# Attention into feed-forward on one core: the second batch's attention queued from a third of the first feed-forward on, ACT tables loaded ahead of use, three squares moved to Pool

## The chip, the cores and the metric

The kernel runs on 1 core of one Trainium2 chip. The metric is the device time of one execution in microseconds (us), as the median of several runs; lower is better. The profile is taken of one execution. Its span, from the first to the last instruction, is about 1.8 us shorter than the time of the same run. All runs quoted were classed as fast runs. With one core a single run says little about its state, so the granted TensorE clock is given where it matters.

Engines are named as in the profile: PE is TensorE (matmul), PEld its weight loads, ACT is ScalarE, DVE is VectorE, POOL is GpSimd, SP only issues DMAs here. "Batch 0" is the first of eight batches.

## The reference

Squared-relu attention on 8 batches of 12 heads, then RMS norm and a SwiGLU feed-forward on all tokens:

```python
# q, k, v: (8, 12, 448, 64)   w_gate, w_val: (768, 1536)   w_out: (1536, 768)
scores = matmul(q, k.T) / sqrt(64)
attn   = maximum(scores, 0) ** 2 / 448
x      = matmul(attn, v)                     # -> (3584, 768)
rms    = sqrt(mean(x * x, axis=-1) + 1e-6)
xn     = x / rms * rms_g
g      = xn @ w_gate
out    = (g * sigmoid(g) * (xn @ w_val)) @ w_out      # float32
```

## The kernel before

The kernel works batch by batch. It emits the attention and the norm of batch 0 alone; then, for each batch b, the feed-forward of b is the main list of units and the attention and norm of b+1 is the side list. `merge` writes both into one order. The schedule is manual: each engine executes its instructions in the order in which they were emitted, and waits (by semaphores) at the first one whose inputs are missing.

```python
def merge(main, side, head=0.0, tail=0.0):
    # side unit k is emitted once the main list has reached the share
    #   head + (1 - head - tail) * k / n   of its total cost
    ...

# emission of the loads, all from POOL's DMA queue, before any attention:
load("q", 0, ...); load("k", 0, ...); load("v", 0, ...)      # batch 0, in parts
for s in range(4):                       # gate and value weights, 4 slices each
    load_w("g", s)
    load_w("v", s)
for nm in ("q", "k", "v"):               # batch 1
    load(nm, 1)
load_wo(0, 2)
load_wo(1, 2)
# ... (cut)

def scores(b, j, cs):                    # head pair j, two of four chunks c
    # per chunk: two matmuls into psS (2 buffers), then
    #   r = relu(psS)  on ACT (on DVE for some c == 3);  later r = r * r
    eng = nc.gpsimd if square_on(b, j, c) == "pool" else nc.vector
    # the squares are kept in `pending` and emitted by flush() at the next scores()
    # ... (cut)

def attention(b):                        # the side units, in order (b = 0, 1)
    add(0.4, lambda: transposes(b, 0))   # PE transposes q, k of the pair (psT), DVE copies
    for j in range(6):
        add(0.5, scores(b, j, (0, 1)))
        add(0.4, transposes(b, j + 1))   # if j + 1 < 6
        add(1.2, scores(b, j, (2, 3)) and attend(b, j - 1))
    add(0.1, flush)
    add(0.8, attend(b, 5))
    # batch 0 has two keep_busy(2) per pair besides: matmuls on zeros

def norm(b):
    # six matmuls of ones with x*x -> psSS
    nc.scalar.activation(out=rstd[:], in_=psSS[:], func=ACT.Sqrt, ...)
    nc.vector.reciprocal(out=rstd[:], in_=rstd[:])
    for kt in range(6):
        nc.vector.scalar_tensor_tensor(out=xn[:, kt, :], ...)   # x * g * rstd

def ffn(b):      # 12 x (gate psG, value psV: six matmuls each), then the output
    # units psO: 3 pairs of (512, 256 columns) for even b, 4 for odd b
    # ... (cut)

keep_busy(16)
for fn in merge([], attention(0) + [(1.1, lambda: norm(0))]):
    fn()
for b in range(8):
    side = attention(b + 1) + [norm(b + 1)]
    main = ffn(b)
    # loads of batch b + 2 from POOL, DMA transposes of it from SP (cut)
    for fn in merge(main, side, 0.0, 0.15):
        fn()
```

The pieces above are abridged from the kernel; the exact text follows.

Of the kernel before, what the change touches and what calls it, by code (L numbers as in the profile page):

```python
# [8 lines left out]
FP32 = mybir.dt.float32  # L9
# [3 lines left out]
ACT = mybir.ActivationFunctionType  # L13
# [4 lines left out]
def merge(main, side, head=0.0, tail=0.0):  # L18


    total = sum(c for c, _ in main)
    if not main:
        return [f for _, f in side]
    out, done, k = [], 0.0, 0
    n = len(side)
    for c, f in main:
        while k < n and done >= total * (head + (1.0 - head - tail) * k / n):
            out.append(side[k][1])
            k += 1
        out.append(f)  # L30
        done += c
    out.extend(f for _, f in side[k:])
    return out
# [3 lines left out]
def kernel(  # L37
# [11 lines left out]
    nc = tc.nc  # L49
    P = nc.NUM_PARTITIONS  # L50
# [13 lines left out]
    const = ctx.enter_context(tc.tile_pool(name="consts", bufs=1))  # L64
# [20 lines left out]
    def load(nm, b, h0=0, h1=H):  # L85
        runs = nm == "v" or b < PE_T
        if (nm, b) not in ld:
            shape = [PC, H, NCH * D] if runs else [PC, NCH, H * D]
            ld[nm, b] = ldpool.tile(shape, BF16, name=nm + "b", tag=nm + "b")
        t = ld[nm, b]  # L90
        src = src_of[nm][b, h0:h1]
        if runs:
            nc.gpsimd.dma_start(out=t[:, h0:h1, :], in_=src.rearrange("h (p c) d -> p h (c d)", c=NCH))  # L93
        else:
            nc.gpsimd.dma_start(  # L95
                out=t[:].rearrange("p c (h d) -> p c h d", d=D)[:, :, h0:h1, :],
                in_=src.rearrange("h (p c) d -> p c h d", c=NCH),
            )
# [4 lines left out]
    def transpose_dma(b):  # L103
        new_qkT(b)
        for ti, nm in enumerate(("q", "k")):
            for c in range(NCH):
                nc.sync.dma_start_transpose(
                    out=qkT[b][:, :, ti, c * PC : (c + 1) * PC], in_=ld[nm, b][:, c, :]
                )
# [7 lines left out]
    def load_w(which, s):  # L117
        dst, src = {"g": (wg_sb, moe_w_gate), "v": (wv_sb, moe_w_val)}[which]
        nc.gpsimd.dma_start(
            out=dst[:, :, s * FS : (s + 1) * FS],  # L120
            in_=src.rearrange("(kt p) f -> p kt f", p=P)[:, :, s * FS : (s + 1) * FS],
        )

    def load_wo(s, n):
        w = FT // n
        nc.gpsimd.dma_start(
            out=wo_sb[:, s * w : (s + 1) * w, :],
            in_=moe_w_out.rearrange("(fk p) m -> p fk m", p=P)[:, s * w : (s + 1) * w, :],
        )
# [14 lines left out]
    masks.make_identity(nc, ident[:])  # L144
    eps_col = const.tile([P, 1], FP32, name="eps_col", tag="eps_col")
    nc.vector.memset(eps_col[:], eps)
    g_sb = wpool.tile([P, KT], FP32, name="g_sb", tag="rmsg")
    nc.sync.dma_start(out=g_sb[:], in_=moe_rms_g.rearrange("(kt p) -> p kt", p=P))
    load("q", 0, 2, 6)
# [5 lines left out]
    for s in range(NSL):  # L155
        load_w("g", s)
        load_w("v", s)
    for nm in ("q", "k", "v"):
        load(nm, 1)
    load_wo(0, 2)  # L160
    load_wo(1, 2)


    xTs = {}

# [18 lines left out]
        return "dve" if c == 3 and (b or j % 2) else "act"  # L184

    def square_on(b, j, c):
        return "dve"

    def flush():
        while pending:  # L190
# [2 lines left out]
    def scores(b, j, cs):  # L193
        pss = []
        for c in cs:
            psS = ps_s.tile([PC, 2, 512], FP32, name="psS", tag="psS")
            for hh in range(2):
                prt = slice(hh * D, (hh + 1) * D)
                nc.tensor.matmul(  # L199
                    out=psS[:, hh, :S],  # L200
                    lhsT=qkT[b][prt, j, 1, c * PC : (c + 1) * PC],
                    rhs=qkT[b][prt, j, 0, :],
                    start=True,
                    stop=True,
                )
            pss.append(psS)
        squares = []
        for c, psS in zip(cs, pss):
            r = apool.tile([PC, 2, S], BF16, name="r", tag="r")
            if relu_on(b, j, c) == "dve":  # L210
                nc.vector.tensor_relu(out=r[:], in_=psS[:, :, :S])  # L211
            else:
                nc.scalar.activation(out=r[:], in_=psS[:, :, :S], func=ACT.Relu)  # L213
            eng = nc.gpsimd if square_on(b, j, c) == "pool" else nc.vector
            squares.append(
                lambda r=r, eng=eng: eng.tensor_tensor(out=r[:], in0=r[:], in1=r[:], op=ALU.mult)  # L216
            )
            rsq[b, j, c] = r
        flush()
        pending.extend(squares)  # L220
# [25 lines left out]
    def attention(b):  # L246
        units = []

        def add(cost, *fns):
            units.append((cost, lambda: [f() for f in fns]))  # L250

        if b < PE_T:
            add(0.4, lambda: transposes(b, 0))
        for j in range(HP):
            add(0.5, lambda j=j: scores(b, j, (0, 1)))
            if b < PE_T and j + 1 < HP:
                add(0.4, lambda j=j: transposes(b, j + 1))
            if b == 0:
                add(0.3, lambda: keep_busy(2))
            add(1.2, lambda j=j: scores(b, j, (2, 3)), lambda j=j: j and attend(b, j - 1))  # L260
            if b == 0:
                add(0.3, lambda: keep_busy(2))
        add(0.1, flush)
        add(0.8, lambda: attend(b, HP - 1), flush)
        return units
# [4 lines left out]
    def norm(b):  # L270
        psSS = ps_m.tile([P, S], FP32, name="psSS", tag="mm")
        for kt in range(KT):
            nc.tensor.matmul(  # L273
                out=psSS[:], lhsT=ones_bf[:], rhs=x2s[b][:, kt, :],
                start=(kt == 0), stop=(kt == KT - 1),
            )
        rstd = npool.tile([P, S], FP32, name="rstd", tag="rstd", bufs=1)
        nc.scalar.activation(  # L278
            out=rstd[:], in_=psSS[:], func=ACT.Sqrt, scale=1.0 / float(DM), bias=eps_col[:]
        )  # L280
        nc.vector.reciprocal(out=rstd[:], in_=rstd[:])  # L281
        xn = npool.tile([P, KT, S], BF16, name="xn", tag="xn")
        for kt in range(KT):
            nc.vector.scalar_tensor_tensor(  # L284
                out=xn[:, kt, :], in0=xTs[b][:, kt, :], scalar=g_sb[:, kt : kt + 1], in1=rstd[:],
                op0=ALU.mult, op1=ALU.mult,
            )
        xns[b] = xn
        if b % 2 == 0:
            hTs[b // 2] = hpool.tile([P, FT, 2 * S], BF16, name="hT", tag="hT")  # L290
# [49 lines left out]
    def ffn(b):  # L340
        units = []
        for fb in range(FT):
            units.append((1.13, lambda fb=fb: gate(b, fb)))
            units.append((1.13, lambda fb=fb: value(b, fb)))
        full = S // P
        for t in range(full) if b % 2 == 0 else range(full, NT):
            units.append((2.56, lambda t=t: outproj(b // 2, t, 0, 512)))
            units.append((1.28, lambda t=t: outproj(b // 2, t, 512, DM - 512)))
        return units

    keep_busy(16)
    for fn in merge([], attention(0) + [(1.1, lambda: norm(0))]):
        fn()
    for b in range(B):
        side = []
        if b + 1 < B:
            side = attention(b + 1) + [(1.1, lambda b=b: norm(b + 1))]
        main = ffn(b)
        if b + 2 < B:
            for nm in ("q", "k", "v"):  # L360
                load(nm, b + 2)
            at = len(main) * 2 // 3
            main[at:at] = [(0, lambda b=b: transpose_dma(b + 2))]
        for fn in merge(main, side, 0.0, 0.15):
            fn()


# [28 lines left out]
```

## Time and profile before

| | before |
|---|---|
| time, median of 3 runs | 487.74 us (487.48 to 487.85) |
| span of the profiled run (its time 487.05) | 485.3 us |
| PE busy | 459.0 us |
| psSS of norm 0 starts | 32.91 us |
| first gate matmul (psG) starts | 48.62 us |
| granted PE clock 0.5 or falling to it | 38.0 to about 51.8 us |

The page's first part gives busy time by engine, with the share of the span and the number of instructions:

```profile
PE 459.0 (95%) x2856; PEld 220.2 (45%) x2872; DVE 284.2 (59%) x452; ACT 253.8 (52%) x372; POOL 50.8 (10%) x45
```

PE is the engine that bounds the kernel. The table of windows of the kernel before shows where it is not yet full. Its columns are the window, its length, then for each engine the busy us and the number of instructions, the granted clock as a share of full speed (PEclk), the DMA share and the GB/s that DMA moved:

```profile
38.00:39.00 1.00, 0.00 (x0) 0.00 (x0) 0.96 (x2) 0.00 (x0) 0.61 (x1) 0.57 1.32 200
...
51.00:52.00 1.00, 1.00 (x5) 0.40 (x3) 0.00 (x0) 0.54 (x1) 0.00 (x0) 0.60 1.15 208
...
200.00:300.00 100.00, 99.68 (x601) 48.04 (x603) 63.11 (x98) 56.30 (x84) 11.09 (x6) 1.00 0.89 98
```

PE is 99.7% busy from 200 to 300 us, and the page's 40 slices show it at 90% or more everywhere between 50 us and the tail. Between 34.4 and 48.1 us it has a gap of nearly 14 us, with one group of transposes in it, and the clock falls to half. The timeline of the kernel before shows what it waits for. The columns are start us, duration us, engine, source line, operation, output <- inputs, shapes, count, and in brackets the engine's idle time just before and what ended it:

```profile
32.91 1.47 PE L273 MATMUL psSS<-x_276,ones_bf 128*128 128x448 bf16 x6
...
33.57 1.28 ACT L278 ACT_TABLE_LOAD   x1
...
34.87 0.63 ACT L278 ACTIVATE rstd<-psSS,eps_col 128x448 f32<-128x448 f32 x1
...
35.53 2.95 DVE L281 RECIPROCAL rstd<-rstd 128x448 f32<-128x448 f32 x1 [1.56 <-ACT rstd L278]
...
38.52 3.66 DVE L284 SCALAR_TENSOR_TENSOR xn<-xT,g_sb,rstd 128x448 bf16<-128x448 bf16 x6
...
44.60 0.59 PE L173 MATMUL psT<-ident,qb 112*64 112x112 bf16 x8 [10.22 <-DMA qb<-in_q_dram]
...
48.10 0.58 PE L173 MATMUL psT<-ident,kb 112*64 112x112 bf16 x8 [2.92 <-DMA kb<-in_k_dram]
...
48.62 2.42 PE L295 MATMUL psG<-xn,wg_sb 128*128 128x448 bf16 x6
```

The chain of norm 0 is psSS on PE, Sqrt on ACT (with a table load of 1.28 us in front), the reciprocal and the six xn on DVE. It is done at 38.52 + 3.66 = 42.2 us. Yet the first psG starts at 48.62, because the transposes of batch 1 (psT) stand before it in PE's order, and their q and k land at 44.6 and 48.1 us. The data for the gate lay ready for 6 us, and its first part for 9.5 us.

The list of waits of PE up to 130 us (us in total, times, longest) says the same. It also shows that waits between the score matmuls and their relus were short:

```profile
PE psT L173 <- DMA qb<-in_q_dram: 10.2, 1, 10.2
PE psT L173 <- DMA kb<-in_k_dram: 3.6, 2, 2.9
PE psS L199 <- ACT r L213: 2.6, 8, 0.4
```

### The profile page before, as it was taken

The page shows a single profiled execution, that of the slowest core. Times are in us where ns is not written, and L with a number is a line of the kernel's source. Part 1 is how long each engine was busy: PE and PEld are TensorE (multiplying, and loading weights), DVE is VectorE, ACT ScalarE, POOL GpSimd, SP SyncE. Part 2 cuts the span into 40 slices and gives each one's busy share as a digit, 9 for nine tenths or more (in the row PEclk, how much of TensorE's full clock was granted, in tenths as well). Part 3 has the DMA queues.
Part 4 walks back from the last instruction along what each step waited for, and adds up shares of the span by engine and source line. Part 5 has one row for each costly group of instructions (what it writes and reads, how often), then busy time and mean ns, then how long its engine had stood idle before and what let it go on. Part 6 is the DMA issues. An engine that isn't in the chain of part 4 may idle for free.

```text
span 485.3 us, 7083 instructions
## 1 busy us (share of the span) xinstructions
PE 459.0 (95%) x2856; PEld 220.2 (45%) x2872; DVE 284.2 (59%) x452; ACT 253.8 (52%) x372; POOL 50.8 (10%) x45
## 2 busy tenths in 40 slices
PE   7960999999999999999999999999999999999995
PEld 3420444444445544454445544454445544455553
DVE  3874477656663676755663576765664577662310
ACT  4870455555654566547654566547554566543221
POOL 8323001140002200040001200000000000000000
PEclk9995899999999999999999999999999999999999
DMA  9999999999301990099501993067101300021013
GB/s 110 202 204 199 209 160 131 113 168 172 44 1 37 197 179 5 1 124 196 62 1 35 190 160 33 1 122 125 23 1 34 97 2 0 1 65 34 0 34 97
DMA packets 128032, 43.32 MB, mean 89 GB/s; under 512 B 100608, under 2 KB 124416, under 8 KB 128000
## 3 DMA queue, kind: packets, MB, share of 16 engines
q0 software_dynamic: 88944, 23.60, 50.5%
q1 hardware_dynamic: 39056, 19.28, 21.6%
q8 instruction: 22, 0.36, 0.3%
q14 instruction: 10, 0.08, 0.1%
HBM read 47.19 MB, written 11.01 MB: 120 GB/s over the span
## 4 chain that ended last, share of the span: by engine, by line
PE 86%; DMA 8%; POOL 1%; DVE 1%; ACT 1%; issue 1%; POOLq 0%
PE psG L295 24%; PE psV L295 23%; PE psO L321 21%; PE psS L199 9%; PE psAV L228 8%; DMA kb<-in_k_dram 5%; DMA wv_sb<-in_moe_w_val_dram 3%; PE psSS L273 1%; DVE xn L284 1%; PE psT L173 1%; DVE rstd L281 1%; POOL kb L93 0%; POOL qb L93 0%; ACT r L213 0%; POOL vb L93 0%
## 5 line engine op out<-in xcount | busy, mean ns | idle before, releaser
L213 ACT ACTIVATE r<-psS 112x896 bf16<-112x896 f32 x147 | 128.5, 915 | 47.1 <-PE psS L199 44.0
L295 PE MATMUL psG<-xn,wg_sb 128*128 128x448 bf16 x576 | 127.0, 356 | 0.9 <-DVE xn L284 0.9
L295 PE MATMUL psV<-xn,wv_sb 128*128 128x448 bf16 x576 | 125.4, 354 | 0.0
L312 DVE TENSOR_TENSOR hT<-sil,psV 128x448 bf16<-128x448 bf16 x96 | 59.6, 621 | 99.0 <-PE psV L295 78.1
L321 PE MATMUL psO<-wo_sb,hT 128*128 128x256 bf16 (+1 forms) x656 | 111.5, 325 | 1.2 <-issue 0.5
L216 DVE TENSOR_TENSOR r<-r 112x896 bf16<-112x896 bf16 x192 | 110.0, 618 | 0.3 <-ACT r L213 0.2
L306 ACT ACTIVATE sil<-psG 128x448 bf16<-128x448 f32 x96 | 52.3, 545 | 87.3 <-PE psG L295 87.0
L321 PEld LDWEIGHTS <-hT 128*128 128x128 bf16 x672 | 64.8, 98 | 47.4 <-issue 3.9
L295 PEld LDWEIGHTS <-wv_sb 128*128 128x128 bf16 x576 | 54.2, 98 | 57.9 <-issue 10.8
L295 PEld LDWEIGHTS <-wg_sb 128*128 128x128 bf16 x576 | 51.9, 98 | 62.4 <-issue 18.9
L328 ACT COPY ost<-psO 128x512 f32<-128x512 f32 (+1 forms) x56 | 26.8, 479 | 81.1 <-PE psO L321 81.1
L199 PE MATMUL psS<-qkT 64*112 64x448 bf16 x384 | 57.6, 372 | 3.3 <-ACT r L213 2.6
L211 DVE TENSOR_SCALAR r<-psS 112x896 bf16<-112x896 f32 x45 | 48.9, 1088 | 17.4 <-PE psS L199 17.4
L228 PE MATMUL psAV<-r,vb 112*64 112x448 bf16 x384 | 46.1, 359 | 0.8 <-DVE r L216 0.8
L281 DVE RECIPROCAL rstd<-rstd 128x448 f32<-128x448 f32 x8 | 23.6, 2953 | 22.6 <-ACT rstd L278 22.6
L199 PEld LDWEIGHTS <-qkT 64*112 64x112 bf16 x384 | 18.0, 124 | 39.1 <-issue 36.3
L239 ACT ACTIVATE xT<-psAV 128x448 bf16<-128x448 f32 x48 | 26.2, 545 | 10.3 <-PE psAV L228 7.0
L93 POOL DMA_DIRECT2D vb<-in_v_dram x9 | 8.1, 903 | 211.0 <-PE psAV L228 156.6
L284 DVE SCALAR_TENSOR_TENSOR xn<-xT,g_sb,rstd 128x448 bf16<-128x448 bf16 x48 | 29.3, 681 | 0.3
L228 PEld LDWEIGHTS <-vb 112*64 112x64 bf16 x384 | 17.7, 109 | 24.6 <-issue 16.7
L95 POOL DMA_DIRECT2D qb<-in_q_dram x6 | 13.8, 2306 | 35.5 <-DMA qkT<-kb 32.7
L178 DVE COPY qkT<-psT 128x896 bf16<-128x896 bf16 x12 | 7.5, 621 | 15.7 <-PE psT L173 15.7
(42 smaller groups left out, 121.7 us busy)
## 6 DMA issues: line engine op xcount, KB each, us to landing
qb<-in_q_dram POOLq DMA_DIRECT2D x7, 672.0 KB, 14.2
kb<-in_k_dram POOLq DMA_DIRECT2D x7, 672.0 KB, 22.5
vb<-in_v_dram POOLq DMA_DIRECT2D x7, 672.0 KB, 9.2
out_dram<-ost SPq DMA_DIRECT2D x8, 336.0 KB, 4.4
wg_sb<-in_moe_w_gate_dram POOLq DMA_DIRECT2D x4, 576.0 KB, 18.8
wv_sb<-in_moe_w_val_dram POOLq DMA_DIRECT2D x4, 576.0 KB, 20.5
wo_sb<-in_moe_w_out_dram POOLq DMA_DIRECT2D x2, 1152.0 KB, 28.8
out_dram<-ost SPq DMA_DIRECT2D x8, 288.0 KB, 4.9
```

Of the source, the lines that this page charges most:

```text
L199: nc.tensor.matmul(out=psS[:, hh, :S], lhsT=qkT[b][prt, j, 1, c * PC : (c + 1) * PC], rhs=qkT[b][prt, j, 0, :], start=True, stop=True,)
L211: nc.vector.tensor_relu(out=r[:], in_=psS[:, :, :S])
L213: nc.scalar.activation(out=r[:], in_=psS[:, :, :S], func=ACT.Relu)
L216: lambda r=r, eng=eng: eng.tensor_tensor(out=r[:], in0=r[:], in1=r[:], op=ALU.mult)
L228: nc.tensor.matmul(out=psAV[hh * D : (hh + 1) * D, :], lhsT=ld["v", b][:, 2 * j + hh, c * D : (c + 1) * D], rhs=rsq[b, j, c][:, hh, :], st ...
L281: nc.vector.reciprocal(out=rstd[:], in_=rstd[:])
L284: nc.vector.scalar_tensor_tensor(out=xn[:, kt, :], in0=xTs[b][:, kt, :], scalar=g_sb[:, kt : kt + 1], in1=rstd[:], op0=ALU.mult, op1=ALU.mult,
L295: nc.tensor.matmul(out=ps[:], lhsT=w_sb[:, kt, fb * P : (fb + 1) * P], rhs=xns[b][:, kt, :], start=(kt == 0), stop=(kt == KT - 1),)
L306: nc.scalar.activation(out=s[:], in_=psG[:], func=ACT.Silu)
L312: nc.vector.tensor_tensor(out=hTs[b // 2][:, fb, o : o + S], in0=sil[b, fb][:], in1=psV[:], op=ALU.mult)
L321: nc.tensor.matmul(out=ps[:, :w], lhsT=hTs[i][:, fk, t * P : (t + 1) * P], rhs=wo_sb[:, fk, o : o + w], start=(fk == 0), stop=(fk == FT - 1),)
L328: nc.scalar.copy(out=ost[:, o : o + w], in_=ps[:, :w])
```

## The change

The intent: PE should not meet the second batch's transposes before their data is there, the Sqrt and Silu tables of ACT should be in place when they are needed, and DVE should be relieved in attention 0. The loads of batch 1 and of the output weights are issued behind attention 0.

```diff
+    def act_table(func):
+        nc.scalar.activation(out=scrap[:], in_=eps_col[:], func=func)
+    act_table(ACT.Sqrt)                       # at the start
@@ loads @@
-    for nm in ("q", "k", "v"):                # from here ...
-        load(nm, 1)
-    load_wo(0, 2)
-    load_wo(1, 2)
@@ square_on @@
-        return "dve"
+        return "pool" if b == 0 and j >= 3 and c == 1 else "dve"
@@ norm, after Sqrt @@
+        act_table(ACT.Silu)
@@ after attention(0), norm(0) @@
+    for nm in ("q", "k", "v"):                # ... to here
+        load(nm, 1)
+    load_wo(0, 2)
+    load_wo(1, 2)
@@ feed-forward @@
-        for fn in merge(main, side, 0.0, 0.15):
+        for fn in merge(main, side, 0.3 if b == 0 else 0.0, 0.15):
```

(`scrap` is a 128x1 tile; its declaration is cut.) With g, v for the gate and value units, T for the transposes, S0(0,1) for the first two score chunks of pair 0, A for attend (the matmuls psAV of squares and v), N for the norm and o for output units, the order that `merge` gives in the first feed-forward is:

```
before: T0 g0 v0 S0(0,1) g1 T1 v1 ... g10 S4(2,3)+A3 v10 g11 S5(0,1) v11 S5(2,3)+A4 o0a fl o0b A5 o1a N o1b o2a o2b
after:  g0 v0 ... g5 T0 v5 S0(0,1) g6 T1 S0(2,3) ... v10 S3(2,3)+A2 S4(0,1) g11 T5 v11 S4(2,3)+A3 o0a S5(0,1) S5(2,3)+A4 o0b fl A5 o1a N o1b o2a o2b
```

More of the change, by code (lines that the diff above doesn't have):

```diff
@@ L146 @@
     nc.vector.memset(eps_col[:], eps)
+    scrap = const.tile([P, 1], FP32, name="scrap", tag="scrap")
+    def act_table(func):
+        nc.scalar.activation(out=scrap[:], in_=eps_col[:], func=func)
+    act_table(ACT.Sqrt)
     g_sb = wpool.tile([P, KT], FP32, name="g_sb", tag="rmsg")
```

## The prediction

> **What bounds the kernel now.** The page gives TensorE (PE) 459.0 of 485.3 us busy (95%); the table of windows shows it 99.7% busy from 110 us to the tail, so only the first 50 us can give much. The timeline of PE shows the hole: psSS ends at 34.4 us, the first gate matmul (psG) starts at 48.62. The xn it needs was complete at 42.2 (table load 33.57-34.85, sqrt 0.63, reciprocal 2.95, six xn at 0.61). PE stands at the second batch's transposes, queued ahead of the gate: the list of waits has psT <- DMA qb 10.2 us and psT <- DMA kb 2.9. In the hole the granted clock falls to 0.5 (38 to 51.7 us), so the first psG group takes 2.42 and psV 1.78, where 1.24 is usual.
>
> **What the change does.**
> 1. head 0.3: the first side unit (T0) moves from before gate 0 to after gate 5. PE then waits for xn only. Weights have landed (slice 0 at 21-24 us), and q, k of batch 1 (44.6, 48.1) come before T0 is reached (about 55). The loads keep their order; moved behind attention 0 they are issued at about 31-36 us, while four weight slices are still in flight: no loss.
> 2. Sqrt table ahead: takes away 1.28 us, but it overlapped psSS; sqrt started 0.45 after psSS ended. Worth 0.4. The Silu load was not critical.
> 3. Three squares (0.56-0.62 us on DVE) go to Pool. DVE is full in attention 0, ACT nearly too (3.9 us per head pair). A Pool square is about 2 us by my estimate (896 elements x 2.6 cycles; the Trainium skill, GPSIMD Engine Reference, § Elementwise); by SBUF — State Buffer, § Who interferes with whom, a DVE op with two SBUF inputs and a reading Pool op exclude each other. No trace shows it yet. I count 0.2 gained, +-0.6.
>
> **Sum.** xn[0] is ready at about 38.5, the first psG group ends at about 41.9 instead of 51.04: -9.15. The batch-1 transpose (0.5) is still to be done, the slow psV (0.5) falls away: these cancel. Given back:
> - Clock: PE idles about 4.3 us, then runs at xn's pace. Before, the clock fell 3.6 us after the hole began. I expect it to fall more often than not: +1.3 on average (0 to 2.5).
> - Density: attention 1 is squeezed into 55% of the first feed-forward. DVE goes from about 65% to 90% there, and the order puts S3(2,3)/S4(0,1) and S5(0,1)/S5(2,3) back to back. With two psS buffers, two relus of 0.84 on ACT (1.09 on DVE) must end first: stalls of about 0.3 and 1.7; the last attend waits about 0.6 for its squares. Before had 0.3 in all: +2.0.
>
> 487.7 - 9.15 + 1.3 + 2.0 = 481.9. From 110 us on nothing changes but the start; the 1.2 us idle at norm 1 stays.
>
> **Time:** 482.0 us, 478.8 to 485.2 eight times in 10. Faster by over 2% 0.10, within 2% 0.88, slower 0.02.
>
> **What would show it.** First psG at 38-39 us, its matmuls spaced 0.61; no wait of psT for DMA; waits psS <- ACT r and psAV <- DVE r of 2-3 us between 80 and 95 us; no table load at 33 us; everything after norm 1 about 6 us earlier. Pool squares of about 2 us, neighbouring DVE squares longer than 0.62.
>
> **What would make it wrong.** Clock stays up and no stalls: about 478.5. Pool squares far slower, so that the last attend waits: up to 3 us back. q1 or k1 landing after 55 us: a new DMA wait. More DVE backlog: 1-3 us more.

## The result

| | before | after |
|---|---|---|
| time, median | 487.80 us of 4 (487.48 to 488.68) | 481.86 us of 4 (481.56 to 482.07) |
| ratio | | 0.9875 (0.9858 to 0.9892) |
| span of the profiled run | 485.3 us | 480.2 us |
| first psG starts | 48.62 us | 38.83 us |
| first psV starts | 50.83 us | 42.13 us |
| psS of batch 2 starts (the first feed-forward is over) | 106.66 us | 101.59 us |

A ratio is the mean time of one kernel's runs over that of the other's of the same rounds, with a 95% interval, so it is not quite the ratio of the medians quoted. The interval shows a gain of 1.1 to 1.4%.

The page after, PE's busy time:

```profile
PE 462.3 (96%) x2872; PEld 220.8 (46%) x2872; DVE 284.5 (59%) x449; ACT 253.7 (53%) x380; POOL 55.7 (12%) x48
```

The timeline after (columns as before; the kernel has a few more lines, so the line numbers are higher by 1 or 2):

```profile
25.42 1.68 POOL L217 TENSOR_TENSOR r<-r 112x896 bf16<-112x896 bf16 x1 [2.22 <-ACT r L214]
25.51 3.14 DVE L217 TENSOR_TENSOR r<-r 112x896 bf16<-112x896 bf16 x3
...
32.92 1.47 PE L274 MATMUL psSS<-x_270,ones_bf 128*128 128x448 bf16 x6
...
34.43 0.63 ACT L279 ACTIVATE rstd<-psSS,eps_col 128x448 f32<-128x448 f32 x1 [0.86 <-PE psSS L274]
...
35.10 2.95 DVE L283 RECIPROCAL rstd<-rstd 128x448 f32<-128x448 f32 x1 [1.11 <-ACT rstd L279]
...
38.09 3.66 DVE L286 SCALAR_TENSOR_TENSOR xn<-xT,g_sb,rstd 128x448 bf16<-128x448 bf16 x6
38.83 3.51 PE L297 MATMUL psG<-xn,wg_sb 128*128 128x448 bf16 x6 [4.43 <-DVE xn L286]
...
42.13 2.45 PE L297 MATMUL psV<-xn,wv_sb 128*128 128x448 bf16 x6
...
44.37 1.92 PE L297 MATMUL psG<-xn,wg_sb 128*128 128x448 bf16 x6
...
46.13 1.30 PE L297 MATMUL psV<-xn,wv_sb 128*128 128x448 bf16 x6
```

psSS starts at the same time as before, 32.92. The Sqrt starts right at its end, without a table load. The first psG no longer waits for a DMA: its six matmuls take 3.51 us because they follow the six xn. Then psV and the second psG take 2.45 and 1.92 us where 1.30 is usual, at half clock. The windows of the granted clock after:

```profile
39.00:40.00 1.00, 0.89 (x2) 0.10 (x1) 1.00 (x3) 0.00 (x0) 0.00 (x0) 0.50 1.40 201
45.00:46.00 1.00, 1.00 (x5) 0.46 (x4) 0.31 (x1) 0.00 (x0) 0.81 (x1) 0.69 1.45 197
46.00:48.00 2.00, 2.00 (x12) 1.01 (x11) 0.47 (x1) 0.54 (x1) 1.46 (x1) 1.00 1.46 198
```

The list of waits of PE after:

```profile
PE psG L297 <- DVE xn L286: 5.3, 5, 4.4
PE psS L200 <- ACT r L214: 3.5, 8, 1.0
...
PE psT L174 <- DMA kb<-in_k_dram: 0.9, 2, 0.7
```

psT waits for DMA have gone from 13.8 to 0.9 us, and a wait of psG for xn of 5.3 us has come (4.4 of it before the first matmul). psS <- ACT has grown by 0.9 us. The timeline of PE after, near the end of the squeezed attention, shows where:

```profile
78.30 0.84 PE L200 MATMUL psS<-qkT 64*112 64x448 bf16 x4
...
86.15 0.59 PE L200 MATMUL psS<-qkT 64*112 64x448 bf16 x4
87.72 0.40 PE L200 MATMUL psS<-qkT 64*112 64x448 bf16 x2 [0.97 <-ACT r L214]
88.52 0.40 PE L200 MATMUL psS<-qkT 64*112 64x448 bf16 x2 [0.41 <-ACT r L214]
...
91.14 0.94 PE L229 MATMUL psAV<-r,vb 112*64 112x448 bf16 x6
92.24 0.38 PE L229 MATMUL psAV<-r,vb 112*64 112x448 bf16 x2 [0.15 <-DVE r L217]
```

S4(0,1), straight behind S3(2,3)+A2, takes 0.84 instead of 0.59 us. S5(2,3), straight behind S5(0,1), waits 0.97 and 0.41 us for relus. The last attend takes 1.41 us (91.14 to 92.55) instead of 0.88, waiting for squares. In the kernel before, the same place has only 0.16:

```profile
91.53 0.40 PE L199 MATMUL psS<-qkT 64*112 64x448 bf16 x2 [0.16 <-ACT r L213]
...
96.74 0.95 PE L228 MATMUL psAV<-r,vb 112*64 112x448 bf16 x8
```

**Ledger of the two profiled runs.** The start of the first psV moves by 50.83 - 42.13 = 8.70 us. From there to the psS of batch 2, after takes 59.46 us and before 55.83. The difference of 3.63 is made of these parts: 1.73 because psV 0 and psG 1 take 4.00 instead of 2.27 us (the 2.27 is measured in the run `warm` below); less 0.47, because before's own psV was slow as well (1.71 instead of 1.24); 0.52 for T0, which before had done already; and the rest, 1.85, for the squeeze. The three places of the squeeze, read singly, give 0.25 + 1.22 + 0.53 = 2.0. From there to the end both take the same (378.6 us).

### The profile page after: what moved, and what is told of

Same layout as the page of the kernel before. It is cut to its first block, busy times and chain, and to the rows that moved or that the text cites. A ratio compares the mean times of both kernels' runs of the same rounds, so it can differ in the third digit from the quotient of the medians.

```text
span 480.2 us, 7118 instructions
## 1 busy us (share of the span) xinstructions
PE 462.3 (96%) x2872; PEld 220.8 (46%) x2872; DVE 284.5 (59%) x449; ACT 253.7 (53%) x380; POOL 55.7 (12%) x48
## 4 chain that ended last, share of the span: by engine, by line
PE 89%; DVE 6%; ACT 2%; issue 1%; DMA 1%; POOL 0%; DVEq 0%; ACTq 0%; POOLq 0%
PE psG L297 24%; PE psV L297 24%; PE psO L323 22%; PE psS L200 9%; PE psAV L229 8%; PE psSS L274 2%; DVE r L217 2%; DVE xn L286 2%; DVE rstd L283 1%; ACT r L214 1%; DMA kb<-in_k_dram 1%; DVE r L212 1%; PE psT L174 1%; PE psB L139 0%; ACT rstd L279 0%
## 5 line engine op out<-in xcount | busy, mean ns | idle before, releaser
L297 PE MATMUL psG<-xn,wg_sb 128*128 128x448 bf16 x576 | 128.4, 357 | 5.7 <-DVE xn L286 5.3
L323 PE MATMUL psO<-wo_sb,hT 128*128 128x512 bf16 (+1 forms) x672 | 113.1, 326 | 0.0
L95 POOL DMA_DIRECT2D qb<-in_q_dram x6 | 13.8, 2304 | 33.2 <-DMA qkT<-kb 32.1
L95 POOL DMA_DIRECT2D kb<-in_k_dram x6 | 15.1, 2511 | 7.5 <-PE psV L297 6.4
## 6 DMA issues: line engine op xcount, KB each, us to landing
qb<-in_q_dram POOLq DMA_DIRECT2D x7, 672.0 KB, 13.8
```

Source lines behind the costliest of these rows:

```text
L95: nc.gpsimd.dma_start(out=t[:].rearrange("p c (h d) -> p c h d", d=D)[:, :, h0:h1, :], in_=src.rearrange("h (p c) d -> p c h d", c=NCH),)
L297: nc.tensor.matmul(out=ps[:], lhsT=w_sb[:, kt, fb * P : (fb + 1) * P], rhs=xns[b][:, kt, :], start=(kt == 0), stop=(kt == KT - 1),)
L323: nc.tensor.matmul(out=ps[:, :w], lhsT=hTs[i][:, fk, t * P : (t + 1) * P], rhs=wo_sb[:, fk, o : o + w], start=(fk == 0), stop=(fk == FT - 1),)
```

## The experiments

All runs below gave correct results. Each lists its edit, the expectation, and what was measured; "before" is the kernel before, run in the same rounds on the same chip. Its median was 488.04 us (486.57 to 489.13) in the first four runs, 487.54 (487.22 to 489.05) in the next four, and 487.57 (486.60 to 488.58) in the last two. Runs of different calls are compared by their ratios, and by distances within the trace.

The theory: what the change wins, it wins by PE's order alone; the clock and the squeeze give part of it back; tables are worth about 0.4 us and the Pool squares next to nothing. Rivals: the shorter chain of attention 0 and norm 0 carries half of the gain; the slow groups come from weights or DMA, not from the clock; density costs nothing.

### head_off: the change without its order

```diff
-        for fn in merge(main, side, 0.3 if b == 0 else 0.0, 0.15):
+        for fn in merge(main, side, 0.0, 0.15):
```

> The kernel after, with the second batch's attention queued from the start again (head 0.0); table loads, Pool squares and the later place of the loads kept. Theory (the order of PE's queue is the change's whole effect): PE stands again at the transpose for batch 1's k, first gate matmul at 47.5 to 49 us, time 487.0 to 488.0, ratio to before 0.998 to 1.001. Rival (the shorter chain of attention 0 and norm 0, by tables and Pool, brings the gain): 483 to 485 us.

Measured: 488.05 us (486.93 to 489.16, 6 runs), ratio 1.0001 (0.9982 to 1.0020): the expected band was missed by 0.05 at its top, and the rival's is far away. The first gate matmul, expected at 47.5 to 49 us, started at 49.48. The timeline of PE of head_off:

```profile
48.96 0.59 PE L174 MATMUL psT<-ident,kb 112*64 112x112 bf16 x8 [2.96 <-DMA kb<-in_k_dram]
49.48 2.42 PE L297 MATMUL psG<-xn,wg_sb 128*128 128x448 bf16 x6
51.69 2.45 PE L297 MATMUL psV<-xn,wv_sb 128*128 128x448 bf16 x6
```

Tables and Pool squares alone bring nothing, because PE stands at the transposes until k of batch 1 lands, whatever the chain of norm 0 does.

### head_only: the order without the rest

```diff
@@ in the kernel before @@
-        for fn in merge(main, side, 0.0, 0.15):
+        for fn in merge(main, side, 0.3 if b == 0 else 0.0, 0.15):
```

> The kernel before with head 0.3 for the first feed-forward as its only edit; loads, tables and squares as before. Theory: nearly the whole gain, 482.0 to 482.8 us (0.4 lost for the Sqrt table on the chain, Pool worth 0 to 0.4), first gate matmul at 39 to 39.5 us. Rival (tables and Pool carry half): 484.5 or more.

Measured: 482.96 us (482.71 to 483.00, 5 runs), ratio 0.9898 (0.9883 to 0.9913), and the first gate matmul at 39.66 us: the band was missed by 0.16 us, the start by 0.16. The timeline of PE of head_only:

```profile
39.66 3.51 PE L295 MATMUL psG<-xn,wg_sb 128*128 128x448 bf16 x6 [4.88 <-DVE xn L284]
```

About 5 of the 6 us come from the order alone; the rival's "half" is refuted. The start is later than after's by 0.83 us, 0.38 of it already at psSS (33.30 instead of 32.92).

### pool_off: all squares on DVE

```diff
-        return "pool" if b == 0 and j >= 3 and c == 1 else "dve"
+        return "dve"
```

> The kernel after with all squares on DVE again. Theory (a Pool square and the DVE squares exclude each other, the swap is about neutral): 481.6 to 482.4 us. Rival (DVE was the limit and the swap saves 0.5 us per head pair): 483.0 or more. Third (the swap costs time, a DVE square grew to about 1.8 us in the trace): 481.2 or less.

Measured: 482.43 us (481.70 to 483.14, 5 runs), ratio 0.9886 (0.9869 to 0.9903). The time is in the first theory's band; its interval overlaps with that of after, so the times alone don't tell 0.5 us from none. The traces do: from the attend of pair 1 to psSS it is 33.55 - 18.14 = 15.41 us here, 32.91 - 17.50 = 15.41 before, and 32.92 - 17.75 = 15.17 after. The three moved squares are worth 0.24 us together in this trace of after. In the other traces the same distance is 15.41 in all with squares on DVE (head_only, early_q1, early_best) and 15.00 to 15.01 in five with Pool squares (head_off, tables_off, warm, head_02, warm_head02_tail02), so 0.4 us is the usual worth. The fence of after above shows why it is not 3 x 0.6: the DVE square that starts at 25.51, next to the Pool square of 25.42, belongs to a group of three that takes 3.14 us. Taken singly, that first square took 2.07 us instead of 0.62 and ended 0.48 us after the Pool square did; the timeline of DVE of after, in a narrow window:

```profile
25.51 2.07 DVE L217 TENSOR_TENSOR r<-r 112x896 bf16<-112x896 bf16 x1
```

The other two Pool squares ran beside DVE's relus from PSUM, which kept their 1.09 us, and met only the start of a DVE square each. Those squares took 0.75 and 0.67 us, and they too ended 0.48 us after the Pool square (23.69 against 23.21, 31.48 against 31.00).

### warm: PE kept busy through norm 0

```diff
+            psB[0] = ps_m.tile([P, S], FP32, name="psB", tag="mm")   # norm, b == 0
+            fill(22)                              # 22 matmuls on zeros after psSS
@@ project, inside the loop over kt @@
+            if nm == "psG" and b == 0 and fb == 0 and kt < KT - 1:
+                fill(2)
```

> The kernel after with 22 extra matmuls on zeros between psSS of norm 0 and the first gate (about 4.1 us at full clock) and two more between each two matmuls of the first psG, so that PE does not idle. Tests the clock term: theory says the granted clock stays at 1.0, psV 0 takes 1.14 to 1.24 instead of 2.24 and psG 1 1.14 instead of 1.71, so 1.4 to 1.8 us less: 480.1 to 480.5 us. Rival (the slow groups come from something else than the clock, such as weights that land late or the DMA load): no gain, 481.6 to 482.5.

Measured: 480.38 us (480.02 to 480.50, 4 runs), ratio 0.9845 (0.9828 to 0.9862); the mean granted clock of the profiled run is 1.0 (after: 0.992). The timeline of PE of warm:

```profile
34.45 4.32 PE L274 MATMUL psB<-busy_bf,ones_bf 128*128 128x448 bf16 x22
...
42.21 1.29 PE L305 MATMUL psV<-xn,wv_sb 128*128 128x448 bf16 x6
43.34 1.30 PE L305 MATMUL psG<-xn,wg_sb 128*128 128x448 bf16 x6
44.48 1.30 PE L305 MATMUL psV<-xn,wv_sb 128*128 128x448 bf16 x6
```

psV 0 and psG 1 take 44.48 - 42.21 = 2.27 us instead of 4.00. The distance from psSS to the first psV is about the same as after's (9.08 against 9.21 us), so little else moved. The clock term is shown: 1.73 us in the traces, 1.5 in the medians.

### head_02: a smaller squeeze

```diff
-        for fn in merge(main, side, 0.3 if b == 0 else 0.0, 0.15):
+        for fn in merge(main, side, 0.2 if b == 0 else 0.0, 0.15):
```

> The kernel after with head 0.2 instead of 0.3 for the first feed-forward. Its order has one main unit or more between each two score units of batch 1 that stood back to back. Theory (the squeeze of attention 1 gives back about 2 us, by waits of psS for relus and of the last attend for squares): 480.1 to 480.9 us, and in the list of waits psS <- ACT r falls by 1 us or more; k of batch 1 has landed before the first transpose (about 50.5 us). Rival (the give-back is clock alone, density costs nothing): 481.6 to 482.3. A miss by data: psT <- DMA kb over 1 us, then no gain.

Measured: 480.51 us (479.95 to 480.68, 4 runs), ratio 0.9846 (0.9829 to 0.9863). T0 stands behind g3 and starts at 50.38 us with no wait for k. The list of waits of PE of head_02:

```profile
PE psS L200 <- ACT r L214: 2.4, 7, 0.4
```

That is 1.1 us less than after's 3.5 and no more than the kernel before had. Free of the clock's share, the stretch from psV 0 to the psS of batch 2 is 99.60 - 42.41 - 1.06 = 56.1 us here (psV 0 and psG 1 took 3.33, so 1.06 over 2.27), and 59.46 - 1.73 = 57.7 us after. So 1.6 of the 1.85 us of the squeeze are had back by 0.2 instead of 0.3; the last attend still waits for squares.

### early_q1: the data earlier instead of the transposes later

```diff
@@ in the kernel before @@
     for s in range(NSL):
         load_w("g", s)
         load_w("v", s)
-    for nm in ("q", "k", "v"):
-        load(nm, 1)
+        if s == 0:
+            for nm in ("q", "k", "v"):
+                load(nm, 1)
```

> The kernel before, order of PE kept (head 0.0), with the loads of batch 1's q, k, v queued behind the first of the four weight slices instead of behind the last. Theory (the hole of 14 us was PE waiting in order for data that came last; bringing the data earlier is worth as much as taking the transpose out of the way, without squeezing attention 1): no wait of psT for DMA, first gate matmul at 39 to 40 us, 480.2 to 481.4 us, below the kernel after. Rival (DMA is simply full, so what comes earlier delays something else as long): a wait for a weight slice of 5 us or more, 485 or more.

Measured: 479.85 us (479.59 to 480.65, 4 runs), ratio 0.9837 (0.9820 to 0.9855): just below the expected band. The timeline of PE of early_q1:

```profile
34.90 0.39 PE L174 MATMUL psT<-ident,qb 112*64 112x112 bf16 x8
...
39.94 3.42 PE L296 MATMUL psG<-xn,wg_sb 128*128 128x448 bf16 x6 [4.45 <-DVE xn L285]
```

The transposes run at 34.90, inside the hole, and PE's list of waits has no weight slice. It still has psT waits for DMA of 0.8 and 0.3 us, but those are batch 0's, at 8 to 9 us. DMA was busy all along in both orders; what mattered was which bytes came first. This edit of the kernel before, in one place, gains at least as much as the whole change (0.9837 against 0.9875, measured on different chips), with no tables, no Pool squares and no squeeze (its psS <- ACT waits are 2.6 us, as before).

### tables_off: the change without the dummy activations

```diff
-    act_table(ACT.Sqrt)
-        act_table(ACT.Silu)
```

> The kernel after without the two dummy activations. Theory: the Sqrt table load is back on ACT at 33 to 35 us, overlaps psSS all but 0.4 to 0.5 us; 482.2 to 482.6 us. Rival (the whole 1.28 us is on the chain): 483.1 or more.

Measured: 482.98 us (481.96 to 484.62, 6 runs), ratio 0.9898 (0.9879 to 0.9917). The median lies between the two bands and the spread is too wide to tell 0.4 from 1.28 us: by its times the run is inconclusive. The trace is not. The timeline of ACT of tables_off:

```profile
33.98 1.28 ACT L278 ACT_TABLE_LOAD   x1
35.28 0.63 ACT L278 ACTIVATE rstd<-psSS,eps_col 128x448 f32<-128x448 f32 x1
```

The load is back, and from the start of psSS to the first psG it is 39.67 - 33.32 = 6.35 us instead of 38.83 - 32.92 = 5.91. The load ahead is worth 0.44 us; the rest of it was hidden behind psSS. Only norm 0's Sqrt load is moved: at norm 1, the trace of after still has one (1.28 us at 95.96).

### warm_head02_tail02: the terms together

The edit of warm, and:

```diff
-        for fn in merge(main, side, 0.3 if b == 0 else 0.0, 0.15):
+        for fn in merge(main, side, 0.2 if b == 0 else 0.0, 0.2 if b == 0 else 0.15):
```

> The run warm (no idle of PE in norm 0) with head 0.2 and, for the first feed-forward only, tail 0.2, which puts norm 1 one unit earlier, ahead of four output units instead of three. Theory: warm's 480.4, less 1.5 to 2 of density stalls, less 1.2 to 1.5 of PE pacing by xn at norm 1: 476.8 to 477.8 us, faster than both kernels. If the terms do not add: 478.5 or more.

Measured: 477.21 us (476.63 to 477.35, 5 runs), ratio 0.9779 (0.9762 to 0.9795): faster than both kernels, and in the expected band. The terms add. After, the pace of xn at norm 1 (one matmul each 0.6 us) stretches psS and psG to 104.81 - 101.59 = 3.22 us up to psV; the timeline of PE of warm_head02_tail02 has the same in 99.95 - 98.28 = 1.67:

```profile
98.28 0.59 PE L200 MATMUL psS<-qkT 64*112 64x448 bf16 x4
98.80 1.31 PE L305 MATMUL psG<-xn,wg_sb 128*128 128x448 bf16 x6
99.95 1.30 PE L305 MATMUL psV<-xn,wv_sb 128*128 128x448 bf16 x6
```

### early_best: the early loads with the same repairs

early_q1's load order and head 0.0, with tables, the fill of warm (19 matmuls, since T0 is done in the hole too), tail 0.2 for the first feed-forward, squares on DVE. The part of the edit that moves the loads and the merge:

```diff
+        if s == 0:                                # behind the first weight slice
+            for nm in ("q", "k", "v"):
+                load(nm, 1)
-        for fn in merge(main, side, 0.3 if b == 0 else 0.0, 0.15):
+        for fn in merge(main, side, 0.0, 0.2 if b == 0 else 0.15):
```

> Batch 1's q, k, v loaded behind the first weight slice (as in early_q1) with head 0.0; tables ahead; PE kept busy in norm 0 as in warm; tail 0.2 for the first feed-forward; squares on DVE. Theory: warm_head02_tail02's 477.2, less 0.3 to 0.5 for the batch-1 transpose done inside the hole and less 0.3 of density, plus 0.2 for no Pool squares: 476.2 to 477.1 us. Rival (nothing is left of the squeeze once head is 0.2): 477.0 to 477.8.

Measured: 476.58 us (476.42 to 479.19, 4 runs), ratio 0.9784 (0.9756 to 0.9811). Three of the four runs lie at 476.4 to 476.7; the fourth, 479.19, has a mean granted clock of 0.991 where the three have 0.997 to 1.0, so its clock fell somewhere; it has no trace. The median is the lowest of all and in the expected band, but the interval covers that of warm_head02_tail02, so which of the two is faster stays open.

### loads_back: the loads in their old place, squares on Pool

```diff
@@ the kernel after, the four load lines moved back ahead of attention 0 @@
```

> The kernel after with the loads of batch 1's q, k, v and of the output weights back in their old place in Pool's program, ahead of attention 0 and so ahead of Pool's squares. Theory (moving the loads is worth nothing itself, it only keeps the squares from standing behind Pool's waits for queue room): the first Pool square starts after the last load issue, at 33 to 34 us instead of 21.5, the attend of pair 3 waits 8 to 10 us for it, 489.5 to 493 us, slower than before. Rival (Pool's issue does not wait, or the place does not matter): 481.5 to 482.5.

Measured: 493.24 us (491.85 to 493.75, 4 runs), ratio 1.0103 (1.0080 to 1.0126): slower than before, as expected; the median lies 0.24 above the band. The timeline of POOL of loads_back:

```profile
32.98 0.83 POOL L126 DMA_DIRECT2D wo_sb<-in_moe_w_out_dram  x1 [2.07 <-DMA wg_sb<-in_moe_w_gate_dram]
33.82 3.32 POOL L221 TENSOR_TENSOR r<-r 112x896 bf16<-112x896 bf16 x2
```

and its list of waits of PE:

```profile
PE psAV L233 <- POOL r L221: 9.7, 1, 9.7
```

POOL executes in order. Each load issue waits until an earlier DMA of the queue has landed, and the squares stood behind the last of these waits, at 33.82 instead of 21.53 us. Moving the loads wins no time itself (they land in time in both places: head_only has the old place, and its list of waits of PE has no psT wait for DMA); it is what makes Pool squares possible at all.

## Why the prediction was right

The time was predicted as 482.0 us (478.8 to 485.2), most probably within 2%; measured were 481.86 us and a ratio of 0.9875. Point by point:

- **The hole and its cause: right.** head_only and head_off show that the order of PE carries 5 of 6 us and that nothing else carries any of it alone; early_q1 shows that the late data and the order are two sides of one cause.
- **Start of the gate stream, "-9.15": measured -8.70.** xn[0] was ready for psG at 38.83, not at 38.5. The 0.2 us that I counted for Pool did come (0.24, and 0.4 in five other traces), but psSS did not start earlier, since attention 0 of the profiled run had lost as much before the first Pool square: the first attend matmuls of pair 1 started 0.25 us later than before (17.75 against 17.50), behind a transpose that had waited 0.67 us for batch 0's k.
- **Clock, "+1.3 on average (0 to 2.5)": measured +1.73**, shown by warm. That is one execution: the same two groups cost 0.84 (pool_off), 0.91 (tables_off), 1.06 (head_02), 1.57 (loads_back) and 1.95 us (head_only) over 2.27 in the other traces in which the gate stream starts the same way, 1.3 on average with after's, so the guess of an average was good, though the clock fell in all six, not only "more often than not". The before's slow psV, counted as 0.5, was 0.47, and the transpose, counted as 0.5, was 0.52.
- **Density, "+2.0": measured +1.85** in the ledger, and at the three places named: S3/S4 0.25 (predicted 0.3), S5 1.4 (1.7), the last attend 0.5 (0.6). But the prediction's own parts don't add up to its 2.0: 0.3 + 1.7 + 0.6 - 0.3 is 2.3. Each part was somewhat too large (the three measured 2.16 before 0.16 is taken off), and the slip in the sum made up for it: that the total agrees this well is partly luck.
- **Tables, "0.4": measured 0.44.** The guess that the load mostly overlapped psSS was right.
- **Pool square "about 2 us": measured 1.68**, with one neighbouring DVE square stretched to 2.07 and two to 0.75 and 0.67.
- **No DMA loss: right.** The wait of psT for k after is 0.9 us, in attention 0 (before 8.54 and 16.43 us), not at T0.

One more agreement is partly luck. The ledger of the two profiled runs gives 5.1 us of span, while the medians differ by 5.9: the profiled run of before (487.05 us) was faster than its median. I took a difference between traces off a median. Within the traces the gain at the start was over-predicted by 0.45 us and the clock's give-back under-predicted by 0.43, so the span fell by 5.1 where the sum said 5.85; the slower median of before hid this. Runs of the kernel before spread over 2.6 us (486.57 to 489.13), those of warm, where the clock stays up until the tail, over 0.5. That the spread comes from the length of the slow-clock stretch is supported by the record, though no run tests it: psV 0 took 1.78 us in the profiled run of before and 2.45 in that of head_off, at the same place of the same PE order. Read from windows of 1 us, the clock was at 0.5 from 38.1 to 51.8 us in before (13.7 us) and from 37.8 to 54.9 in head_off (17.1); it was so for 6.8 us in after (38.8 to 45.6) and 10.2 in head_only (36.7 to 46.9). All four are whole multiples of about 3.4 us, so the same PE order came out one such step apart in two executions. And of the 29 runs of before beside the experiments, 13 had a mean granted clock of 0.980 and took 487.74 to 489.13 us, 10 had 0.986 and took 486.57 to 488.07 (this mean counts a fall in the tail too, so it is a hint and no proof).

## What to carry to other kernels

An engine that executes in order stops at the first instruction whose data is late, so look behind a long wait for work whose inputs are ready: either take the late one out of the way or let its data come first, and prefer the latter if the other order squeezes work elsewhere. Cost a moved piece of work at its new place too: here 3.6 of 8.7 us came back as half clock and as relus without room, and both could be repaired once they were named. Before moving compute to the engine that also issues DMAs, look at what that engine waits for in its own order.

## What the Trainium skill lacked or had wrong

- "GPSIMD Engine Reference", § 3.1 Elementwise — side-by-side cycle accounting, gives about 2.6 cycles per element for a two-input op (my estimate: 1.94 us for 896 elements). The page's measured case is fp32; the trace has 1.68 us for 112x896 bf16, in all three cases.
- "SBUF — State Buffer", § Who interferes with whom, says that a DVE instruction with two SBUF inputs and a GpSimd instruction that reads SBUF exclude each other. The trace agrees: a DVE square took 2.07 instead of 0.62 us beside a Pool square, while DVE relus from PSUM kept 1.09. The page has no figure for this pair.
- "ScalarE: Activation LUTs", § What ACT_TABLE_LOAD costs, gives about 1283 ns for the load and about 1380 ns of drain, 2.66 us for a switch. The load agrees (1.28 us); no drain shows here: in tables_off xT ends at 33.96, the load runs from 33.98 to 35.26, and the Sqrt starts at 35.28, so the switch cost 1.3 us.
- "TensorE: Matmul & The Clock Gate", Part 1, gives a free-running window of about 3.4 us and a fall of the clock after an idle one. The traces agree on the window: the slow stretches of 6.8, 10.2, 13.7 and 17.1 us are two to five times 3.4. They don't agree that a whole window must be idle: in head_only the clock fell at 36.7 us, 1.9 us after psSS ended at 34.78, so the last 3.4 us before the fall held the 1.48 us of psSS. The page has no figure for matmuls paced one by one by another engine: here the clock stayed at 0.5 through the six psG matmuls at 0.6 us each and returned 3.5 us after the dense stream began (42.1 to 45.6 us). In warm, matmuls on zeros in the same gaps held it at 1.0.
- I found no page that says that a DMA issue on POOL's queue waits for an earlier DMA of that queue to land, and so holds back the compute emitted behind it. In before's trace each issue from the thirteenth to the last of the weights waits for the DMA issued eight before it (the third gate slice at 11.91 us for the first part of v); in loads_back this cost 9.7 us in one wait. Whether the limit is the hardware's or set by the program's semaphores is not shown.
